# Attention products in pairs, one-tile requests for w_out, and earlier q loads in a fused attention and feed-forward kernel on one Trainium2 core

## The chip, the cores and the metric

The kernel runs on one core of one Trainium2 chip. The metric is the device time of one execution in microseconds (us). Six executions of the kernel before took 951.77 to 955.05 us, with a median of 954.17 us.

The core's engines work side by side and each follows its own list in order: TensorE (PE, whose weight loads are listed as PEld) multiplies matrices, VectorE (DVE) and ScalarE (ACT) do elementwise work, and SyncE's queue (SP) hands out transfers to 16 DMA engines.

## The reference

```python
kv  = einsum('bhsd,bhse->bhde', k, v)            # 8 batches, 8 heads, 576 tokens, 64 wide
out = einsum('bhsd,bhde->bhse', q, kv)
rms = sqrt(mean(out * out, axis=-1) + 1e-6)
x   = (out / rms * g_norm) -> 4608 tokens x 512  # heads side by side
h   = x @ w_in                                   # 512 -> 2048
g   = s * max(h, 0)**2 + b
y   = g @ w_out                                  # 2048 -> 512
```

Everything is float32.

## The kernel before

**Units, chunks, steps.** The 4608 tokens are 36 chunks of 128. Four chunks make a unit of 512 tokens, so there are nine units, u = 0 to 8. For a unit the kernel computes the first matrix product (`mm1`, with w_in) in four steps s = 0 to 3 of 512 hidden columns each, and then the second (`mm2`, with w_out). Both use a Strassen-Winograd scheme: seven products in place of eight, with sums before and after. In a step the seven products are called `x1`, `z2`, `x6`, `y7`, `x5`, `x3`, `y4`. They stand in this order on TensorE, except that `x3` and `y4` of a step are written in the next step: `x1(s)`, `x3(s-1)`, `z2(s)`, `y4(s-1)`, `x6(s)`, `y7(s)`, `x5(s)`. Each is 8 rows of 128 x 256 in the trace. `x1`, `x6`, `x5` and `x3` of a step add up in one PSUM bank, and between them ScalarE copies the running sum out (`keep`, L587: r1 after `x1`, r2 after `x6`, r4 after `x5`; after `x3` it takes a ReLU, L618). So `x6` can't start before r1 is copied, `x5` not before r2, `x3` not before r4. `y7` and `y4` add up in a bank with the tag "y", of which there are two. VectorE adds and squares: after `z2`, after `y4` and after `x5` an addition (L247) and a squared ReLU (L542), after `x3` a square (L621), a sum and a difference. r2 has one buffer, which the addition after `y4(s-1)` has to read before r2 of step s is copied.

For u above 1 the second product has two levels of this scheme. `rest()` writes it out: `p1`, `p2`, `p6`, `p7`, `p4` are second-level products of seven small ones each (numbered 1, 2, 6, 7, 5, 3, 4), `x5_of` and `x3` products of one level. After each small product VectorE scales and adds (`scaled`, L702); product 6 adds to the bank of product 1 and waits until VectorE has read that bank.

**Attention beside it.** While unit u is multiplied, the four chunks of unit u+1 go through attention in parts, each put at a place (s, n) of the steps by `sides(u)`. The places are: n = 0 before `x1`, 1 after `z2`, 2 after `x6`, 3 before `x5`. The parts of a chunk are `turn` (VectorE transposes q, L409), `product` (32 rows of the form 128*32 on TensorE, L439, then the square on ScalarE, L448, and the row sum on VectorE, L450), `norm` (root on ScalarE, L454; reciprocal and multiplication on VectorE, L456 and L458, the latter out of PSUM) and `turn_x` (transpose on VectorE, L483; for every second chunk also the scaling of two chunks by g_norm, four ScalarE instructions, L489). A product has its own PSUM bank (`ps_a`, one buffer). In the units 3 to 7 one chunk a step has its parts at the step's places; the last one has them at (2,3) to (3,2). In unit 2 the fourth chunk's parts fall into `rest()`, at the places `at(0)`, `at(1)`, `at(2)`.

`kv_product` computes k^T v of one batch (144 rows of the form 64*64, L377, into both "t" banks, then four ScalarE copies, L392). One is due in each of the units 1 to 6, at place (1,3).

**Transfers.** Nearly all are issued by SP's queue, in written order. `pump(n)` asks for the next n tiles of w_out (or of k and v) into a ring of seven buffers (L671, L674, L115); each waits until the buffer's last reader is done. `loads` asks for q of two chunks of unit u+2 (L1198) in 16 to 48 pieces. In the units from 3 on, the first half stands at (1,3), behind `kv_product` and its `pump(4)`, and the second at (3,1). Results are stored at L806.

## Time and profile before

| what | value |
|---|---|
| median of 6 executions | 954.17 us (951.77 to 955.05) |
| the profiled execution, its own time | 953.78 us |
| its span | 952.0 us |
| PE / PEld busy | 936.4 us (98%) / 837.7 us (88%) |
| DVE / ACT busy | 643.5 us (68%) / 191.8 us (20%) |
| unit 2, from its first `x1` to the next unit's | 102.25 us |
| units 3, 4, 5, 6, 7 | 102.03, 101.03, 101.07, 101.10, 97.00 us |
| granted TensorE clock in these units | 1.00 |

Times in the timeline count from the span's start. A line gives the start, the busy time, the engine, the source line, the operation, what is written and read, the shape, how many instructions are taken together, and in brackets how long the engine was idle before and what ended that. Unit 2 starts at 247.02 us, unit 3 at 349.27, unit 4 at 451.30, unit 5 at 552.33, unit 6 at 653.40, unit 7 at 754.50.

### The profile page before, as it was taken

The numbers are of one execution on the slowest core, as the hardware profiler recorded it, in microseconds if no ns is written. First come the engines' busy times: TensorE is split into PE (matmuls) and PEld (weight loads), VectorE is DVE, ScalarE is ACT, GpSimd is POOL, SyncE is SP. The second block draws the span as 40 slices with busy tenths as digits, with TensorE's granted clock in tenths as the row PEclk, the third lists the DMA queues.
The fourth block names the chain that finished last, engine by engine and source line by source line (L and its number), as shares of the span: only waits on it lengthen the run. The fifth ranks groups of instructions, "written<-read, shape, count | busy, mean of one in ns | idle before, by whom it ended". The sixth has DMA issues, their size and how long they took to land.

```text
span 952.0 us, 17809 instructions
## 1 busy us (share of the span) xinstructions
PE 936.4 (98%) x7270; PEld 837.7 (88%) x7270; DVE 643.5 (68%) x1167; ACT 191.8 (20%) x366; POOL 6.7 (1%) x18
## 2 busy tenths in 40 slices
PE   7999999999999999999999999999999999999997
PEld 6888888888888998899889988999889988998997
DVE  2789767486567865776568665775578667854684
ACT  2773132101121103200231013101320032001100
POOL 2000000000000000000000000000000000000000
PEclk9999999999999999999999999999999999999999
DMA  9688827578762767165644764375526520653064
GB/s 255 194 283 250 280 78 195 138 218 263 208 174 49 219 184 215 24 196 187 177 108 132 240 181 106 98 240 165 157 52 218 185 90 12 209 181 121 13 221 143
DMA packets 136656, 158.46 MB, mean 166 GB/s; under 512 B 77696, under 2 KB 91776, under 8 KB 136448
## 3 DMA queue, kind: packets, MB, share of 16 engines
q1 hardware_dynamic: 133472, 155.57, 55.1%
q10 hardware_dynamic: 2784, 1.77, 0.8%
q8 instruction: 57, 0.93, 0.4%
q14 instruction: 23, 0.19, 0.1%
q0 software_dynamic: 320, 0.00, 0.0%
HBM read 131.34 MB, written 25.95 MB: 165 GB/s over the span
## 4 chain that ended last, share of the span: by engine, by line
PE 91%; DVE 5%; DMA 2%; ACT 1%; issue 1%; SPq 0%; ACTq 0%; DVEq 0%
PE x_ps L91 41%; PE y_ps L91 27%; PE z_ps L91 9%; PE t_ps L91 8%; PE x_ps L439 3%; PE kv_ps L377 2%; DMA w_raw<-in_moe_w_in_dram 1%; DMA kv_sb<-in_k_dram 1%; DVE sub L250 1%; DVE a L250 1%; DVE b_row L247 1%; DVE xn L458 0%; DMA w_sb<-w 0%; DVE xT L483 0%; ACT w_raw L227 0%
## 5 line engine op out<-in xcount | busy, mean ns | idle before, releaser
L587 ACT COPY r<-x_ps 128x512 f32<-128x512 f32 x96 | 56.2, 586 | 433.9 <-PE x_ps L91 392.2
L91 PE MATMUL y_ps<-xs,wb 128*128 128x256 f32 x512 | 122.3, 382 | 0.3 <-DVE a L247 0.3
L91 PE MATMUL x_ps<-xs,ws 128*128 128x256 f32 x512 | 122.1, 381 | 0.0
L91 PEld LDWEIGHTS y_ps<-xs,wb 128*128 128x128 f32 x512 | 95.7, 190 | 15.1 <-issue 2.4
L91 PEld LDWEIGHTS x_ps<-xs,ws 128*128 128x128 f32 x512 | 96.4, 190 | 14.0 <-issue 1.0
L247 DVE TENSOR_TENSOR a<-y_ps,r 128x512 f32<-128x512 f32 x64 | 44.1, 689 | 76.2 <-ACT r L587 71.3
L91 PE MATMUL x_ps<-xT,wa 128*128 128x256 f32 x384 | 90.3, 381 | 0.1
L91 PEld LDWEIGHTS x_ps<-xT,wa 128*128 128x128 f32 x384 | 71.8, 190 | 11.1 <-issue 1.2
L91 PE MATMUL x_ps<-w_sb,a 128*128 128x256 f32 (+1 forms) x376 | 79.6, 364 | 0.0
L91 PEld LDWEIGHTS x_ps<-w_sb,a 128*128 128x128 f32 x376 | 66.8, 190 | 8.3 <-issue 0.4
L542 DVE SCALAR_TENSOR_TENSOR a<-a 128x512 f32<-128x512 f32 x96 | 66.4, 691 | 3.0
L91 PE MATMUL y_ps<-w_sb,sub 128*128 128x128 f32 x504 | 62.0, 275 | 0.0
L91 PE MATMUL x_ps<-xT,ws 128*128 128x256 f32 x256 | 60.8, 380 | 0.0
L91 PEld LDWEIGHTS y_ps<-w_sb,sub 128*128 128x128 f32 x504 | 60.2, 192 | 0.7
L91 PE MATMUL z_ps<-xT,wa 128*128 128x256 f32 x256 | 60.5, 379 | 0.0
L91 PE MATMUL x_ps<-w_sb,s 128*128 128x256 f32 x256 | 57.9, 380 | 0.8 <-DMA w_sb<-w 0.8
L91 PE MATMUL t_ps<-w_sb,sub 128*128 128x128 f32 x448 | 54.7, 275 | 0.4 <-DVE r L702 0.4
L91 PEld LDWEIGHTS z_ps<-xT,wa 128*128 128x128 f32 x256 | 48.6, 190 | 6.6
L91 PE MATMUL y_ps<-w_sb,a 128*128 128x128 f32 (+1 forms) x360 | 54.0, 299 | 0.0
L91 PEld LDWEIGHTS x_ps<-xT,ws 128*128 128x128 f32 x256 | 47.8, 190 | 6.9 <-ACT r L587 0.9
L91 PEld LDWEIGHTS t_ps<-w_sb,sub 128*128 128x128 f32 x448 | 52.8, 192 | 1.0 <-DVE r L702 0.6
L91 PEld LDWEIGHTS x_ps<-w_sb,s 128*128 128x128 f32 x256 | 47.5, 190 | 7.0 <-issue 1.1
(139 smaller groups left out, 1236.3 us busy)
## 6 DMA issues: line engine op xcount, KB each, us to landing
w_sb<-w SPq DMA_DIRECT2D x147, 512.0 KB, 4.8
w_sb<-w SPq DMA_DIRECT2D x35, 256.0 KB, 2.8
w_raw<-in_moe_w_in_dram SPq DMA_DIRECT2D x8, 1024.0 KB, 8.0
w_raw<-in_moe_w_out_dram SPq DMA_DIRECT2D x8, 1024.0 KB, 5.7
w_sb<-in_k_dram SPq DMA_DIRECT2D x48, 144.0 KB, 2.9
w_sb<-in_v_dram SPq DMA_DIRECT2D x48, 144.0 KB, 3.0
out_dram<-o SPq DMA_DIRECT2D x104, 64.0 KB, 2.3
w<-sub SPq DMA_DIRECT2D x20, 256.0 KB, 4.3
```

What stands on the lines that cost most here:

```text
L91: nc.tensor.matmul(o, lhsT=lhsT, rhs=rhs, start=start, stop=stop, skip_group_check=True)
L247: nc.vector.tensor_tensor(out=o, in0=a, in1=b, op=ALU.add)
L250: nc.vector.tensor_tensor(out=o, in0=a, in1=b, op=ALU.subtract)
L377: nc.tensor.matmul(ps[r][l * HB : l * HB + HB, i, :], lhsT=kv[l][rows, 0, j, :], rhs=kv[l][rows, 1, j, :], start=(j == 0), stop=(j == R - 1),)
L439: nc.tensor.matmul(ps[32 * p : 32 * p + 32, w, :], lhsT=st["qT"][:, p, 32 * w : 32 * w + 32], rhs=bd_kv[(b if w < 2 else b1) % 2][:, p, :] ...
L542: nc.vector.scalar_tensor_tensor(t, t, 0.0, t, ALU.max, ALU.mult)
L587: nc.scalar.copy(st[name], src)
```

## The change

It touches the units 2 to 7.

1. The products of two chunks are written directly behind each other. For this the second of a pair gets another PSUM bank: one of tag "t" for the chunks 13 and 15, one of tag "y" from chunk 17 on. Its row sum becomes a part of its own (`row_sum`), placed later.
2. In the units 3 to 6 the first pair stands directly ahead of `kv_product`, which moves from (1,3) to (1,1). In unit 2, `kv_product` moves to (1,1) too, and the first pair stands at (2,0).
3. The other parts move. From unit 3 on, both `turn_x` of the first pair stand at (2,0) and the last chunk's at (3,1), where it was at (3,2). In unit 2 the parts of two chunks, not one, fall into `rest()`; their products stand at (3,2).
4. The halves of q are asked for at (1,0) and (2,0) from unit 3 on, and the first half at (2,0), before (2,2), in unit 2.
5. In `rest()` nearly every `pump(2)` becomes two `pump(1)`, each behind the small product that is the last reader of a tile. The number of tiles is the same (24).

```diff
-        def product():
+        def product(with_sum=True):
...
-                ps = ps_a.tile([P, NP, P], FP32, name="x_ps", tag="x")
+                pool, tag = (ps_a, "x")
+                if c % 2 and c > 12:
+                    pool, tag = (ps_t, "t") if c < 16 else (ps_f, "y")
+                ps = pool.tile([P, NP, P], FP32, name="x_ps", tag=tag)
...
             nc.scalar.activation(st["xn"], st["x"], AF.Square)
+            if with_sum:
+                row_sum()
+
+        def row_sum():
             st["ss"] = attp.tile([P, H], FP32, name="ss", tag="ss")
             nc.vector.reduce_sum(st["ss"], st["xn"], axis=mybir.AxisListType.X)
...
         def rest():
             p1[1]()
             p1[2]()
+            pump(1)
             step["y4"]()
             p1[6]()
             step["y4_square"]()
             p1[7]()
+            pump(1)
             p1[5]()
-            pump(2)
             step["x3"]()
...
             x5_of(1, lambda: p6["sums"]((7, 3)), lambda: p7["sums"]((5, 6, 7)))
+            pump(2)
             at(2)
-            pump(2)
             p6[1]()
...
             y4_of(0, 3)
+            pump(1)
             y4_of(1, 4)
-            pump(2)
+            pump(1)
             at(("q", 2))
...
         first, second = {}, {}
+        if u + 1 < U:
+            turn, product, norm, turn_x, _, row_sum = chunks_of(u + 1)
+            product = [partial(fn, False) for fn in product]
+        kv = [lambda: kv_product(kv_due[u]), lambda: pump(NP)] if u in kv_due else []
+        q = {half: [partial(loads, u + 2, half)] for half in range(2)}
...
-        if u in kv_due:
-            first[1, 3] = [lambda: kv_product(kv_due[u]), lambda: pump(NP)]
-        for *place, unit, half in (
-            [(1, 3, 2, 1)] if u == 1 else [(2, 2, 4, 0)] if u == 2
-            else [(1, 3, u + 2, 0), (3, 1, u + 2, 1)]
-        ):
-            first.setdefault(tuple(place), []).append(partial(loads, unit, half))
...
-        for s in range(NS):
-            j = s if u > 2 else s - 1
-            if j >= 0:
-                places = [(s, n) for n in range(4)] if s < 3 else [(2, 3), (3, 0), (3, 1), (3, 2)]
-                for place, fn in zip(places, (turn, product, norm, turn_x)):
-                    first.setdefault(place, []).append(fn[j])
         if u == 2:
-            first[3, 3] = [turn[3]]
-            second = {0: [product[3]], 1: [norm[3]], 2: [turn_x[3]]}
+            first = {
+                (1, 1): [turn[0], *kv],
+                (1, 3): [turn[1]],
+                (2, 0): [*product[:2], *q[0]],
+                (2, 1): row_sum[:2],
+                (2, 2): norm[:2],
+                (2, 3): turn_x[:1],
+                (3, 0): [turn_x[1], turn[2]],
+                (3, 1): [turn[3]],
+                (3, 2): product[2:],
+            }
+            second = {0: row_sum[2:], 1: norm[2:], 2: turn_x[2:]}
...
+        else:
+            first = {
+                (0, 1): [turn[0]],
+                (0, 3): [turn[1]],
+                (1, 0): q[0],
+                (1, 1): [*product[:2], *kv],
+                (1, 2): [*turn[2:], *row_sum[:2]],
+                (1, 3): norm[:2],
+                (2, 0): [*turn_x[:2], *q[1]],
+                (2, 1): product[2:],
+                (2, 2): row_sum[2:],
+                (2, 3): norm[2:],
+                (3, 0): [turn_x[2]],
+                (3, 1): [turn_x[3]],
+            }
```

## The prediction

> **What bounds the kernel now.** The page says TensorE: busy for 98% of the span and 91% of the chain that ended last. So only time on TensorE's list counts: gaps in it, and waits that the new order adds.

> ```profile
> PE 936.4 (98%) x7270; PEld 837.7 (88%) x7270; DVE 643.5 (68%) x1167; ACT 191.8 (20%) x366; POOL 6.7 (1%) x18
> ...
> PE 91%; DVE 5%; DMA 2%; ACT 1%; issue 1%; SPq 0%; ACTq 0%; DVEq 0%
> ...
> PEld x_ps L439 <- issue: 10.1, 29, 0.8
> ```

> The last line, from the waits, names the change's target: 29 times the weight loads stand still ahead of an attention product, and nothing visible holds them. Next the timeline of weight loads, in unit 5 and where two products already follow each other, early in the kernel.

> ```profile
> 563.80 1.70 PEld L91 LDWEIGHTS x_ps<-xT,ws 128*128 128x128 f32 x8
> 565.52 1.70 PEld L91 LDWEIGHTS z_ps<-xT,wa 128*128 128x128 f32 x8
> 567.56 0.81 PEld L439 LDWEIGHTS x_ps<-bd_kv,qT 128*32 128x32 f32 x32 [0.33 <-issue]
> 568.57 1.59 PEld L91 LDWEIGHTS y_ps<-xs,wb 128*128 128x128 f32 x8 [0.20 <-issue]
> 570.19 1.70 PEld L91 LDWEIGHTS x_ps<-xs,ws 128*128 128x128 f32 x8
> ...
> 573.95 2.42 PEld L377 LDWEIGHTS kv_ps<-w_sb 64*64 64x64 f32 x144 [0.33 <-issue]
> 576.43 1.59 PEld L91 LDWEIGHTS x_ps<-xs,ws 128*128 128x128 f32 x8
> ...
> 24.24 0.81 PEld L439 LDWEIGHTS x_ps<-bd_kv,qT 128*32 128x32 f32 x32 [0.58 <-DVE qT L425]
> 25.03 0.89 PEld L439 LDWEIGHTS y_ps<-bd_kv,qT 128*32 128x32 f32 x32
> 26.12 3.32 PEld L91 LDWEIGHTS x_ps<-xT,wa 128*128 128x128 f32 x16 [0.20 <-ACT xn L448]
> ```

> A product of the steps takes 1.727 us from start to start (563.80 to 565.52), only 1.61 after a gap. With the attention product, 565.52 to 570.19 is 4.67; two step products alone would be 3.45, so it costs 1.2. In the pair, the second starts 0.79 after the first and the next form 1.09 later: 1.88, against 1.01 (567.56 to 568.57) for one. The second costs 0.87, so a pair saves 1.2 - 0.87 = 0.33 us.

> Last, what stands close to the limit on ACT, DVE and SP.

> ```profile
> 602.13 0.59 ACT L587 COPY r<-x_ps 128x512 f32<-128x512 f32 x1 [4.83 <-DVE a L247]
> 603.42 1.71 ACT L489 ACTIVATE xT<-xT,g_col 128x256 f32<-128x256 f32 x4 [0.71 <-DVE xT L483]
> ...
> 599.92 0.69 DVE L542 SCALAR_TENSOR_TENSOR a<-a 128x512 f32<-128x512 f32 x1
> ...
> 603.00 1.70 PEld L91 LDWEIGHTS x_ps<-xs,ws 128*128 128x128 f32 x8
> ...
> 320.05 0.19 DVE L456 RECIPROCAL inv<-rms 128x8 f32<-128x8 f32 x1
> ...
> 325.04 0.30 DVE L702 SCALAR_TENSOR_TENSOR r<-t_ps,s_col,o 128x128 f32<-128x128 f32 x1
> ...
> 325.39 2.75 PEld L91 LDWEIGHTS t_ps<-w_sb,sub 128*128 128x128 f32 x24 [0.60 <-DVE r L702]
> ...
> 374.96 37.39 SPq L1198 DMA_DIRECT2D q_sb<-in_q_dram  x64
> ...
> 412.92 0.85 SPq L674 DMA_DIRECT2D w_sb<-w  x2
> ...
> 416.94 3.32 PEld L91 LDWEIGHTS x_ps<-w_sb,s 128*128 128x128 f32 x16 [0.92 <-issue]
> ```

> In unit 5's last step r2 is copied at 602.13, and `x5` may start at 603.00: 0.28 to spare. In unit 2's `rest()`, VectorE works without a pause from 320.05, and TensorE already waits 0.60 for its 325.04. In unit 3 the 64 pieces of q keep SP until 412.4, and a w_out tile comes late.

> **The change part by part.**

> *Pairs, units 3 to 7.* Ten pairs by 0.33: -3.3 us. The second bank holds nobody up: the other "y" bank was last read a step earlier.

> *kv behind the first pair, units 3 to 6.* Joined, the product's 0.20 and kv's 0.33 fall away, a gap from form 128*32 to 64*64 comes instead, and one short block (1.61 for 1.727, a gain of 0.12) is lost: 0.41 less the new gap. No row shows that gap; the gaps at these forms' ends run from 0.07 (after kv: 573.95 + 2.42 to 576.43) to 0.33, so the saving is 0.08 to 0.34. No gap at all would give 0.41. Nothing excludes a dearer one: at twice 0.33 it is a loss of 0.25. I take a gap of 0.2, as at a product's other exit: 4 x 0.2 = -0.8 (+1.0 to -1.6). [...] Its k and v are issued by 561.4 in unit 5 and land 3.0 later; kv's new place is at about 568.

> *What kv's old place cost.* At (1,3) its copies and the scaling delayed r4: 0.22 of waiting, 0.12 of it regained, four times: -0.35.

> *The order in step 3, units 3 to 7.* The last `turn_x` moves ahead of the addition after `y4`, and its scaling ahead of r2 on ACT. From 599.92 in unit 5's clock: the squared ReLU takes 0.61, the transpose starts at 600.53 and the scaling 0.73 later (as 602.69 to 603.42), at 601.26, until 602.97; r2 then at 603.0 until 603.63. `x5` starts at 603.68 for 603.00. Less 0.12 regained: 0.56, five times: +2.8. Behind `x5` only r4 and the addition queue up; the addition ends at 607.16, and `y4` would start at 607.2.

> *The order in step 2, units 3 to 7.* Both `turn_x` now stand ahead of r1 on ACT, and `y7` takes the bank that `y4` has just left. From the addition after `x5(1)`, 7.85 us after `y4(0)` starts: squared ReLU 0.72 later, two transposes (0.62, 0.64), scaling (0.73, 1.71), r1 and ReLU (0.48, 0.63), square, sum, difference (0.73, 0.72, 0.61), addition and squared ReLU after `z2` (0.72, 0.62), and the addition after `y4(1)`, 0.69: 9.6, so 17.47 after that start. Nine step products and a pair later (2 x 1.61 + 7 x 1.727 + 0.3 + 1.88) `y7` wants the bank at 17.49. I cost this at nothing, with no reserve: every 0.1 more on that chain is 0.1 per unit.

> *Unit 2.* Two pairs for four singles (one of them was in `rest()`): the step part grows by 2 x (1.2 + 0.87) - 3 x 1.2 = 0.5, and the second pair waits about 0.5 for its transposed q, which VectorE reaches behind step 3's sums. The 0.45 that `y4` waited there at 300.64 goes. So `rest()` begins 0.5 later and wins back 1.2, the product that stood there. But VectorE doesn't: one more row sum takes the place of the 0.80 that it waited for the square, so product 6 of `p2`, which waits for VectorE's reading of product 1, starts 0.3 later than before. Then, ahead of the same step in `p6`, one more norm (0.20 + 0.69, starts 0.84 apart) and transpose (0.63) come before 325.04: 0.3 + 1.5 = +1.8 for the whole unit. Afterwards VectorE has 0.4 to spare between products again, and TensorE leads.

> *q sooner.* The same number of pieces at about 0.58 us; SP's idle wait for kv (369.8 to 372.2 in unit 3) is filled by the first half, so the late tile is asked for 2.8 sooner: 0.92 less 0.12: -0.8, or nothing if the release of its buffer held it instead. The four tiles that stand behind the first half come up to 10 us later; their first reader is 25 us away.

> *Tiles one by one.* Nothing: each transfer waits for its buffer's last reader already (SP's waits name `z_ps` 26 times, 118.8 us), and no store stands between the halves of a pair. Ring slots hide it; without them each tile's 4.8 us to land would show.

> Sum: -3.3 - 0.8 - 0.35 - 0.8 + 2.8 + 1.8 = -0.65. The profiled execution took 953.78, 0.4 below the median; the difference goes on the median: 954.17 - 0.65 = 953.5 us.

> **The rivals.**

> 1. *One of the two jams isn't there.* If ACT does the scaling behind r2, 2.8 go; if VectorE's order in unit 2 has slack that I missed, +1.8 becomes -1.0 (two pairs and the 0.45). Either gives about -3.5: 950.7. For it: only starts and spacings of the old order are known. Against: the scaling is written ahead of r2, and ACT runs in order.
> 2. *Neither jam:* -0.65 - 2.8 - 2.8 = -6.3: 947.9. That is what pairing would give if the side engines had room.
> 3. *Slower: `y7` waits for its bank in step 2.* The chain of 9.6 us has 0.02 to spare. From 0.5 us more per unit the sum passes +1.9; at 0.9, it is +3.8: 958.0. For it: a dozen steps in a row without reserve. Against: each is a duration that repeats to 0.02 in every unit.
> [...]

> **How the numbers follow.** About 0.2% (1.9 us) is what a measurement of this kernel tells from no change. My sum 47%, from 952.3 to 956.1; one jam missing 25%; neither 8%; `y7` waiting for 0.5 or more 18%; pairs saving nothing 2%. Faster 0.33, within 0.2% 0.47, slower 0.20. The range reaches from 950.3, past the first rival, to 956.5, into the third; it leaves out the second, and the ends of the third and fourth.

> **What the profile after would show.** Weight loads of L439 0.79 apart in pairs, kv (L377) behind a pair with a gap of 0.1 to 0.3; in step 3 of the units 3 to 7 `x5` behind an ACT copy of r by 0.6 to 0.7; in unit 2 a wait of over 2 us for a VectorE `r` at product 6 of `p6`; no 0.92 in unit 3. Units 4 to 6 would be about 0.4 shorter, unit 7 about equal. I am wrong if these waits are missing, or if `y7` of step 2 shows one.

## The result and the profile after

The kernel after took 958.02 us in the median of 19 executions (954.22 to 963.01); the kernel before, on the same chips, 953.5 us (951.51 to 955.5). The ratio is 1.005, with a 95% interval of 1.004 to 1.006: slower by 0.5%. The forecast was 953.5 us with a range up to 956.5, so the result lies outside it: -0.65 us was forecast, and +4.5 measured. The profiled execution took 961.43 us, with a span of 959.6 (before: 953.78 and 952.0).

These lines of the page and of the waits of the kernel after answer to the first ones shown of before.

```profile
PE 937.4 (98%) x7270; PEld 843.0 (88%) x7270; DVE 639.2 (67%) x1167; ACT 191.7 (20%) x366; POOL 6.7 (1%) x18
...
PE 79%; DVE 9%; DMA 5%; ACT 3%; issue 2%; SPq 1%; ACTq 0%; DVEq 0%
...
PEld kv_ps L377 <- issue: 8.2, 8, 3.1
PEld x_ps L442 <- issue: 4.8, 13, 0.8
PEld x_ps L91 <- ACT r L594: 2.6, 5, 0.5
PEld t_ps L91 <- DVE r L709: 2.0, 1, 2.0
PEld x_ps L442 <- DVE a L628: 1.7, 5, 0.3
...
PEld y_ps L91 <- DVE a L247: 1.3, 2, 1.1
```

The target was hit: idle time ahead of attention products (L442) that names no releaser fell from 10.1 us in 29 waits to 4.8 in 13. Some of it only changed its name (the 1.7 us put down to VectorE's `a` are new); counted over all releasers, 33 waits with 12.1 us became 23 with 9.2. But the busy times hardly moved, and 7.6 us more went by. Two new waits were expected (ACT's r2 ahead of `x5`, VectorE's r in unit 2). One was not: k^T v (L377) stands still for 8.2 us with no semaphore named (before: 4.9), 3.1 at a time.

Unit by unit, from a unit's first `x1` to the next unit's, as read from the weight loads of each profiled execution (in before, unit 6 starts at 653.37, unit 7 at 754.41 and unit 8 at 852.67, so unit 7 is 98.26 long; the 653.40, 754.50 and 97.00 in the section on the profile before are less exact):

```
us          unit 2   unit 3   unit 4   unit 5   unit 6   unit 7
before      102.25   102.03   101.03   101.03   101.05    98.26
after       105.81   101.49   103.64   100.46   104.73    97.97
difference   +3.56    -0.54    +2.61    -0.57    +3.68    -0.29
```

The units 4, 5 and 6 are written alike, and yet two are 3 to 4 us longer than the third. That was the first thing to explain. The weight loads of units 3, 4 and 6 around the joined k^T v:

```profile
366.07 1.69 PEld L442 LDWEIGHTS x_ps<-bd_kv,qT 128*32 128x32 f32 x64 [0.33 <-DVE a L628]
367.96 2.50 PEld L377 LDWEIGHTS kv_ps<-w_sb 64*64 64x64 f32 x144 [0.20 <-issue]
370.53 1.59 PEld L91 LDWEIGHTS y_ps<-xs,wb 128*128 128x128 f32 x8
...
467.56 1.69 PEld L442 LDWEIGHTS x_ps<-bd_kv,qT 128*32 128x32 f32 x64 [0.33 <-DVE a L628]
469.44 2.34 PEld L377 LDWEIGHTS kv_ps<-w_sb 64*64 64x64 f32 x139 [0.20 <-issue]
474.84 0.20 PEld L377 LDWEIGHTS kv_ps<-w_sb 64*64 64x64 f32 x5 [3.06 <-issue]
475.11 1.59 PEld L91 LDWEIGHTS y_ps<-xs,wb 128*128 128x128 f32 x8
...
673.54 1.72 PEld L377 LDWEIGHTS kv_ps<-w_sb 64*64 64x64 f32 x97 [0.20 <-DMA out_dram<-o]
677.80 0.79 PEld L377 LDWEIGHTS kv_ps<-w_sb 64*64 64x64 f32 x47 [2.54 <-issue]
678.65 3.06 PEld L91 LDWEIGHTS y_ps<-xs,wb 128*128 128x128 f32 x8
```

In unit 3 the join looks as forecast: 0.20 between the pair and k^T v, no gap behind it. In unit 4 the 144 rows break off after 139 for 3.06 us, in unit 6 after 97 for 2.54. In unit 4's pause no other engine of the core worked, only transfers went on, as the windows show (columns: length; busy time and instructions of PE, PEld, DVE, ACT, POOL; granted clock, DMA share, GB/s):

```profile
471.80:474.80 3.00, 0.12 (x7) 0.00 (x0) 0.00 (x0) 0.00 (x0) 0.00 (x0) 1.00 0.56 101
678.60:681.80 3.20, 3.20 (x16) 2.52 (x8) 0.00 (x0) 1.04 (x4) 0.00 (x0) 0.50 0.23 36
326.50:331.00 4.50, 4.44 (x25) 4.45 (x26) 1.81 (x5) 1.51 (x4) 0.00 (x0) 0.62 0.21 72
```

The second window, behind unit 6's pause, runs at half the granted clock: the next eight loads take 3.06 instead of 1.59. The third, behind the wait in unit 2's `rest()`, does so for most of its length.

**What TensorE waits for in a pause.** The page's list of DMA queues (packets, MB, share) has rows for instructions, one of them this:

```profile
q8 instruction: 57, 0.93, 0.4%
```

```
kernel after     piece ends at entry ... of the 424    pause
unit 3           71 and 327                            none
unit 4           157 and 413                           3.06 at 413
unit 5           243                                   none
unit 6           73 and 329                            2.54 at 329
```

With two ends inside, one piece of 256 is used up in 2.0 to 2.7 us (from the first end to the second in these three units). In unit 4 the list passes the first end at 469.75, but the records of the instruction queue show the next transfer starting only at 472.24 (it takes 1.18), and TensorE resumes at 474.84, 1.4 behind the transfer's end and 5.1 after the passing. In unit 6 the passing is at 672.66, the transfer at 675.52 (0.94), and the resumption at 677.80, 1.3 and again 5.1 later. In unit 3, with nearly the same alignment as in unit 6, the transfer starts at 367.19, 0.2 after the passing, and there is no pause. Where a single product stands among the steps, a piece lasts 12 us and more in this trace, and no such pause is seen there.

### The profile page after: what moved, and what is told of

It reads as the page before. It is cut to its first block, busy times and chain, and to the rows that moved or that the text cites. A ratio compares the mean times of both kernels' runs of the same rounds, so it can differ in the third digit from the quotient of the medians.

```text
span 959.6 us, 17790 instructions
## 1 busy us (share of the span) xinstructions
PE 937.4 (98%) x7270; PEld 843.0 (88%) x7270; DVE 639.2 (67%) x1167; ACT 191.7 (20%) x366; POOL 6.7 (1%) x18
## 4 chain that ended last, share of the span: by engine, by line
PE 79%; DVE 9%; DMA 5%; ACT 3%; issue 2%; SPq 1%; ACTq 0%; DVEq 0%
PE x_ps L91 36%; PE y_ps L91 22%; PE z_ps L91 8%; PE t_ps L91 8%; PE x_ps L442 3%; DMA w_raw<-in_moe_w_in_dram 2%; PE kv_ps L377 2%; ACT xT L496 1%; DVE b_row L247 1%; DMA kv_sb<-in_k_dram 1%; DVE xT L490 1%; DVE sub L250 1%; DMA w_raw<-in_moe_w_out_dram 1%; DVE a L250 1%; ACT w_raw L222 1%
## 5 line engine op out<-in xcount | busy, mean ns | idle before, releaser
L91 PE MATMUL y_ps<-xs,wb 128*128 128x256 f32 x512 | 124.0, 386 | 0.7 <-DVE a L247 0.7
L91 PE MATMUL x_ps<-xs,ws 128*128 128x256 f32 x512 | 121.6, 380 | 0.6
L91 PEld LDWEIGHTS x_ps<-xs,ws 128*128 128x128 f32 x512 | 96.8, 190 | 15.7 <-ACT r L594 2.6
L91 PEld LDWEIGHTS y_ps<-xs,wb 128*128 128x128 f32 x512 | 96.8, 192 | 15.4 <-DVE a L247 1.3
L247 DVE TENSOR_TENSOR a<-y_ps,r 128x512 f32<-128x512 f32 x64 | 43.8, 685 | 90.2 <-ACT r L594 59.0
L91 PE MATMUL x_ps<-xT,wa 128*128 128x256 f32 x384 | 89.7, 380 | 0.1
L91 PEld LDWEIGHTS x_ps<-xT,wa 128*128 128x128 f32 x384 | 72.3, 190 | 10.3 <-ACT xT L496 0.5
L91 PE MATMUL x_ps<-w_sb,a 128*128 128x256 f32 (+1 forms) x376 | 79.6, 364 | 0.0
L91 PEld LDWEIGHTS x_ps<-w_sb,a 128*128 128x128 f32 x376 | 66.9, 190 | 8.2 <-issue 0.4
L91 PE MATMUL y_ps<-w_sb,sub 128*128 128x128 f32 x504 | 62.1, 275 | 0.6 <-DVE r L709 0.6
L91 PEld LDWEIGHTS y_ps<-w_sb,sub 128*128 128x128 f32 x504 | 60.2, 192 | 1.5 <-DVE r L709 0.8
L91 PE MATMUL x_ps<-xT,ws 128*128 128x256 f32 x256 | 60.5, 379 | 0.0
L91 PE MATMUL z_ps<-xT,wa 128*128 128x256 f32 x256 | 60.5, 379 | 0.0
L91 PE MATMUL t_ps<-w_sb,sub 128*128 128x128 f32 x448 | 56.3, 280 | 1.8 <-DVE r L709 1.8
L91 PE MATMUL x_ps<-w_sb,s 128*128 128x256 f32 x256 | 57.8, 380 | 0.0
L91 PEld LDWEIGHTS t_ps<-w_sb,sub 128*128 128x128 f32 x448 | 54.4, 197 | 2.4 <-DVE r L709 2.0
L628 DVE TENSOR_TENSOR a<-a 128x512 f32<-128x512 f32 x32 | 22.0, 689 | 50.6 <-ACT a L625 50.6
L91 PEld LDWEIGHTS z_ps<-xT,wa 128*128 128x128 f32 x256 | 48.6, 190 | 6.6
L91 PE MATMUL y_ps<-w_sb,a 128*128 128x128 f32 (+1 forms) x360 | 53.7, 298 | 0.0
L91 PEld LDWEIGHTS x_ps<-xT,ws 128*128 128x128 f32 x256 | 48.1, 190 | 6.2
```

The source lines that it names most:

```text
L91: nc.tensor.matmul(o, lhsT=lhsT, rhs=rhs, start=start, stop=stop, skip_group_check=True)
L247: nc.vector.tensor_tensor(out=o, in0=a, in1=b, op=ALU.add)
L628: nc.vector.tensor_mul(ga["a21", s], ga["a21", s], ga["a21", s])
```

## The experiments

All edits are to the lists in `sides(u)`, except where said. Ratios are to the kernel before.

**1. k^T v apart from the pair.** The kernel after, with k^T v of the units 3 to 6 back at (1,3).

```diff
-                (1, 1): [*product[:2], *kv],
+                (1, 1): product[:2],
...
-                (1, 3): norm[:2],
+                (1, 3): [*norm[:2], *kv],
```

> In units 3 to 6 k^T v goes back to its old place ahead of x5 (behind the first pair's norm), so its 144 short products no longer follow the pair; all else stays. Code theory (TensorE's list is brought in pieces of 256 instructions, and pair and k^T v together, 424 short ones in 4.3 us, use two pieces up faster than the next one comes): the pauses of 2.5 to 3.1 us inside k^T v in units 4 and 6 go, and with them the clock's dip in unit 6; the median falls by 2.5 to 4 us, to 954 to 955.5, and executions lie closer together than the 9 us of the changed kernel. Unit-2 theory (all is lost in unit 2's order): k^T v alone moves nothing but the joint's 0.2 per unit: 958 to 959.

Measured: 954.64 us (12 executions, 952.44 to 957.6), ratio 1.0011 (0.9998 to 1.0023), 3.4 below the kernel after. The units 4 to 6 take 100.69, 100.66 and 100.66 us, all alike, and no pause is left in k^T v:

```profile
474.52 2.45 PEld L377 LDWEIGHTS kv_ps<-w_sb 64*64 64x64 f32 x144 [0.33 <-DMA q_sb<-in_q_dram]
477.04 1.59 PEld L91 LDWEIGHTS x_ps<-xs,ws 128*128 128x128 f32 x8
```

The lines are from unit 4's weight loads. So the join costs 3.4 us (3.7 by the two ratios to before), where the forecast had it save 0.8 plus 0.35. A joined unit without a pause, unit 5 of the kernel after, is 0.20 shorter (100.46): the saving is there, and the pauses cost many times as much. In the same run unit 2 takes 104.21 us (1.96 more than before), with the same wait of 2.0 in `rest()`, but the clock stays at 1.00 through the unit:

```profile
247.19:351.39 104.20, 101.32 (x842) 91.59 (x842) 71.17 (x135) 16.82 (x36) 0.00 (x0) 1.00 0.57 162
```

**2. Unit 2 in its old order.** The kernel after, with unit 2's single products, row sums and `rest()` parts at the places of before, and no bank of tag "t".

```diff
-                if c % 2 and c > 12:
-                    pool, tag = (ps_t, "t") if c < 16 else (ps_f, "y")
+                if c % 2 and c > 16:
+                    pool, tag = (ps_f, "y")
...
+            each = [lambda p=p, r=r: (p(), r()) for p, r in zip(product, row_sum)]
...
-                (1, 1): [turn[0], *kv],
-                (1, 3): [turn[1]],
-                (2, 0): [*product[:2], *q[0]],
...
-                (3, 2): product[2:],
+                (1, 0): [turn[0]],
+                (1, 1): [each[0]],
+                (1, 2): [norm[0]],
+                (1, 3): [*kv, turn_x[0]],
+                (2, 0): [turn[1]],
+                (2, 1): [each[1]],
+                (2, 2): [*q[0], norm[1]],
+                (2, 3): [turn_x[1], turn[2]],
+                (3, 0): [each[2]],
...
-            second = {0: row_sum[2:], 1: norm[2:], 2: turn_x[2:]}
+            second = {0: [each[3]], 1: [norm[3]], 2: [turn_x[3]]}
```

> Unit 2 has the old order, with single products, and all from unit 3 on is as in the changed kernel. Unit-2 theory: 3.5 us or more come back (unit 2 takes 105.8 us in the changed kernel's profile, 102.25 in the old one's), median 953.5 to 954.5. Code theory: only the waits of unit 2 go, 1.8 that I worked out and 0.6 for a late q, in some executions 1.6 for a clock dip: median 955 to 956, and the pauses in k^T v of units 3 to 6 stay.

Measured: 954.85 us (12 executions, 952.44 to 957.15), ratio 1.0003 (0.999 to 1.0017). The median lies between the two theories' ranges, but both have their part: unit 2 takes 102.28 us, so its pairs cost some 3 us as the kernel after has them, and the pauses stay. The list is one entry longer here (14,762): in unit 4 the break comes after 138 rows for 1.94, in the units 3 and 6 for about half a microsecond.

```profile
466.01 2.34 PEld L377 LDWEIGHTS kv_ps<-w_sb 64*64 64x64 f32 x138 [0.20 <-issue]
470.29 0.20 PEld L377 LDWEIGHTS kv_ps<-w_sb 64*64 64x64 f32 x6 [1.94 <-issue]
```

**3. Both.** Edits 1 and 2 together.

```diff
-                (1, 1): [*product[:2], *kv],
+                (1, 1): product[:2],
...
-                (1, 3): norm[:2],
+                (1, 3): [*norm[:2], *kv],
```

> Both: unit 2 in the old order and k^T v apart in units 3 to 6. Code theory together with unit 2's waits: 952 to 953, that is the pairs' 3.3 us less the five waits of x5 (0.4 each) and the late q of unit 3 (about 1). If both losses were the same one seen twice, this would be no better than the better of the two alone.

Measured: 952.12 us (11 executions, 950.42 to 953.25), ratio 0.9976 (0.9965 to 0.9987). With the two costs gone the rest of the change is a gain of 0.24%. Units 4 to 6 are 100.66 us each.

**4. And the last scaling a place later.** Experiment 3 with the last chunk's `turn_x` back where it was, so that ACT copies r2 first.

```diff
-                (3, 1): [turn_x[3]],
+                (3, 2): [turn_x[3]],
```

> As both, and the last chunk's transpose with its four scalings goes back from (3,1) to (3,2), behind the copy of r2, in units 3 to 7. Theory of the wait: the 0.51 us before x5 in step 3 goes, 0.4 net in five units: 2 us below the run with both, 950 to 951, faster than the kernel before by 0.3%. Rival: the transpose delays the sums of the second product by as much: the same as with both.

Measured: 949.76 us (6 executions, 947.98 to 951.96), ratio 0.9951 (0.9935 to 0.9967): faster than both kernels, and a little below the 950 to 951 that was expected. The window of unit 5's stretch of experiment 3 (columns as above):

```profile
551.87:652.53 100.66, 100.55 (x843) 91.48 (x842) 69.05 (x131) 17.11 (x36) 0.00 (x0) 1.00 0.54 158
```

And the windows of units 5 and 7 here:

```profile
550.41:650.69 100.28, 100.28 (x842) 91.56 (x842) 69.06 (x131) 17.23 (x36) 0.00 (x0) 1.00 0.55 158
750.97:848.55 97.58, 97.58 (x698) 89.20 (x698) 69.04 (x131) 16.20 (x32) 0.00 (x0) 1.00 0.40 128
```

TensorE is busy in all of the 100.28 us. ACT's timeline in step 3 of this unit shows r2 copied before the scaling:

```profile
598.94 0.58 ACT L594 COPY r<-x_ps 128x512 f32<-128x512 f32 x1 [4.58 <-PE x_ps L91]
599.85 1.71 ACT L496 ACTIVATE xT<-xT,g_col 128x256 f32<-128x256 f32 x4 [0.32 <-DVE xT L490]
```

In the weight loads of the same stretch `x5` (600.26) follows `y4` with no wait:

```profile
598.53 1.70 PEld L91 LDWEIGHTS y_ps<-xs,wb 128*128 128x128 f32 x8
600.26 1.70 PEld L91 LDWEIGHTS x_ps<-xs,ws 128*128 128x128 f32 x8
```

**5. The list moved by 84 entries.** If pieces of 256 entries cause the pauses, moving the whole list must move them from unit to unit. The kernel after, with 21 small products (four entries each), whose result nobody uses, early in the kernel.

```diff
+    pad_ps = ps_f.tile([P, 2, TB], FP32, name="pad_ps", tag="z", bufs=1)
+    for i in range(21):
+        g = slice(32 * (i % 4), 32 * (i % 4) + 32)
+        nc.tensor.matmul(pad_ps[g, 0, :P], lhsT=ident[:, g], rhs=ident, start=True, stop=True)
```

> The changed kernel with 21 short products added near its start, whose result nobody uses; they put 84 rows into TensorE's list where the engine waits anyway. Code theory: the ends of the 256-row pieces stand 84 rows earlier in every later burst. In the changed kernel's profile they stand 71 and 327 rows into the burst in unit 3, 157 and 413 in unit 4, 243 in unit 5, 73 and 329 in unit 6, and the pauses were at 413 and 329. Now they should stand at 243 in unit 3, 73 and 329 in unit 4, 159 and 415 in unit 5, 245 in unit 6: a pause can come after 329 rows in unit 4 or 415 in unit 5, none over 0.3 us in units 3 and 6. Median about as the changed kernel, 957 to 959. Rival (a transfer that k^T v or its unit waits for): the pauses stay in units 4 and 6 and at the same products.

Measured: 959.03 us (9 executions, 955.33 to 962.36), ratio 1.0052 (1.0034 to 1.007): no faster, but the pauses are elsewhere, at two of the places that had been named beforehand.

```profile
473.08 1.72 PEld L377 LDWEIGHTS kv_ps<-w_sb 64*64 64x64 f32 x97 [0.20 <-DMA out_dram<-o]
475.15 0.79 PEld L377 LDWEIGHTS kv_ps<-w_sb 64*64 64x64 f32 x47 [0.35 <-issue]
...
573.97 2.35 PEld L377 LDWEIGHTS kv_ps<-w_sb 64*64 64x64 f32 x140 [0.20 <-DMA out_dram<-o]
578.80 0.29 PEld L377 LDWEIGHTS kv_ps<-w_sb 64*64 64x64 f32 x4 [2.48 <-issue]
...
678.58 2.51 PEld L377 LDWEIGHTS kv_ps<-w_sb 64*64 64x64 f32 x144 [0.20 <-DMA out_dram<-o]
```

The ends fall 84 entries earlier: 243 in unit 3, 73 and 329 in unit 4, 159 and 415 in unit 5, 245 in unit 6. Unit 5 now breaks off after 140 rows for 2.48, unit 4 after 97 for only 0.35, and unit 6 runs through. Unit 5 of the kernel after had no pause, and unit 6 had one; the code of neither changed. Two shorter stalls (1.99 and 1.35) came in the units 0 and 1 as well, where k^T v stands without a pair but now has two ends inside; the first of them:

```profile
107.08 2.00 PEld L377 LDWEIGHTS kv_ps<-kv_sb 64*64 64x64 f32 x129 [0.33 <-issue]
111.06 0.32 PEld L377 LDWEIGHTS kv_ps<-kv_sb 64*64 64x64 f32 x15 [1.99 <-issue]
```

**6. The join without pairs.** The kernel before, with k^T v directly ahead of the one product at (1,1) in the units 3 to 6.

```diff
-            first[1, 3] = [lambda: kv_product(kv_due[u]), lambda: pump(NP)]
+            first[1, 3 if u < 3 else 1] = [lambda: kv_product(kv_due[u]), lambda: pump(NP)]
```

> The kernel before with one edit: in units 3 to 6 k^T v stands at (1,1), directly ahead of the second chunk's single product. Code theory: 292 + 64 rows in one burst; where two ends of pieces fall into it 2.5 to 4 us apart there is a pause, so up to 2 us per such unit: median 954 to 956, slower than before by 0.1 to 0.2%, though a gap of the weight loads is saved. Rival (joining as such is good, and only the pair's order costs): 0.2 to 0.3 us saved in each of four units, and 0.1 for the wait of x3: 952.5.

Measured: 954.38 us (12 executions, 951.2 to 959.43), ratio 1.0012 (0.9995 to 1.0028): not told from no change. One unit of four pauses, unit 4 (102.72 us), and this time inside the attention product, after 25 of its 32 rows:

```profile
468.28 0.68 PEld L439 LDWEIGHTS x_ps<-bd_kv,qT 128*32 128x32 f32 x25
470.84 0.15 PEld L439 LDWEIGHTS x_ps<-bd_kv,qT 128*32 128x32 f32 x7 [1.88 <-issue]
```

So the pause belongs neither to the pair nor to k^T v, but to the number of the entry. The units 5 and 6, with one end inside, gain 0.2 to 0.3 us. Unit 3 has two ends inside too (after 2 and 258 of 357 entries) and doesn't pause, so two ends in the burst make a pause possible, not certain.

**All pauses together.** The kernel after and the experiments 2, 5 and 6 have ten pauses that name no semaphore inside a burst of these short products. Counted from the start of each kernel's list, every one of them falls at a multiple of 256 plus 193 or 194. A list has 57 such ends, as many as its instruction queue has transfers; experiment 5's longer list (14,845 entries) has 58 of both. So each transfer can be set beside one end. The columns are times in us: when the list passed the end before, when the transfer that belongs to that end ran, when the list reached the next end, and when TensorE resumed.

```
                 end before   transfer          next end   resumed   behind transfer
after, unit 4      469.75     472.24-473.42      471.78     474.84      1.42
after, unit 6      672.66     675.52-676.46      675.26     677.80      1.34
exp. 2, unit 3     362.95     363.18-364.49      365.57     365.98      1.49
exp. 2, unit 4     466.31     468.00-468.88      468.35     470.29      1.41
exp. 2, unit 6     669.80     669.89-671.55      672.39     672.93      1.38
exp. 5, unit 0     107.21     108.61-109.50      109.07     111.06      1.56
exp. 5, unit 1     162.24     163.36-164.32      164.23     165.58      1.26
exp. 5, unit 4     472.20     472.55-473.69      474.80     475.15      1.46
exp. 5, unit 5     574.28     576.33-577.37      576.32     578.80      1.43
exp. 6, unit 4     466.46     468.41-469.31      468.96     470.84      1.52
```

Whatever the pause's length, TensorE resumes 1.26 to 1.56 us behind the end of that transfer. In all ten the list was at the next end less than 1.2 us behind it; at the 551 other ends of the ten traces (each list's first end left out) it came 1.2 us or more behind it, and there is no such pause at any of them. Unit 3 of experiment 6 is one: its transfer had ended at 363.10, and the list came to the next end at 365.66.

**7. One-tile requests alone.** The kernel before, with `rest()` as the change has it.

```diff
             p1[2]()
+            pump(1)
...
-            pump(2)
+            pump(1)
```

> The kernel before with only the second product's requests one by one, each behind a tile's last reader. My step: nothing, within 0.1% of before (953 to 954.5), since each request waits for its buffer on SP's queue anyway. Rival: the earlier request lets a tile land sooner and takes the 0.92 us wait of unit 3 away: 953.

Measured: 953.86 us (11 executions, 952.25 to 955.11), ratio 1.0002 (0.9993 to 1.001). No cost and no gain can be told from no change. (In the profiled execution unit 3 took 103.39 us, since a second w_out tile came late and TensorE waited 1.28 for it; the median doesn't show it.)

**8. q sooner alone.** The kernel before, with the q requests at (1,1) and (2,3) from unit 3 on, and at (2,0) in unit 2.

```diff
-            [(1, 3, 2, 1)] if u == 1 else [(2, 2, 4, 0)] if u == 2
-            else [(1, 3, u + 2, 0), (3, 1, u + 2, 1)]
+            [(1, 3, 2, 1)] if u == 1 else [(2, 0, 4, 0)] if u == 2
+            else [(1, 1, u + 2, 0), (2, 3, u + 2, 1)]
```

> The kernel before with only q asked for sooner: at (1,1) and (2,3) from unit 3 on, at (2,0) in unit 2. My step: the wait of 0.92 us in unit 3's rest() goes, 0.8 net: 953.0. Rival: the tile was held by its buffer, so nothing: 953.8.

Measured: 953.68 us (11 executions, 951.98 to 956.26), ratio 1.0003 (0.9993 to 1.0012). The expected 953.0 did not come; the late w_out tile of unit 3 stayed late. First the issues of SP's queue:

```profile
379.52 1.82 SPq L671 DMA_DIRECT2D w_sb<-w  x4
...
387.87 23.98 SPq L1198 DMA_DIRECT2D q_sb<-in_q_dram  x48
```

And the weight loads, with the wait that should have gone:

```profile
416.51 3.32 PEld L91 LDWEIGHTS x_ps<-w_sb,s 128*128 128x128 f32 x16 [1.06 <-issue]
```

SP stands from 381.3 to 387.87, waiting for the last `turn` of the old order, at (2,3), to give its q buffer free. The next w_out tile is asked for at 411.95, 63.2 us into the unit, as before (412.44, also 63.2). In the kernel after the transposes come earlier, SP goes on, that tile is asked for 58.5 us into the unit, and the wait is gone. So asking for q sooner alone brings nothing here; what the earlier transposes bring alone was not run.

## Why the prediction was wrong, point by point

**Pairs, -3.3: right.** In the units 3 to 7 of the kernel after, the second product of each of the ten pairs starts 0.79 after the first. Experiment 4 has only these pairs and the other small gains in the units 4 to 7: 100.28 for 101.03 to 101.05, and 97.59 for 98.26. Unit 7 has no k^T v, and its -0.67 is two pairs by 0.33.

**kv behind the first pair, -0.8: this is the step that failed.** I bounded it by gaps between forms, and the gap came out as taken: 0.20 ahead of L377, smaller than the 0.33 that this case's rows reach. A unit without a pause gained the 0.20 of the sum. But the step left out what feeds TensorE: 424 entries in 4.3 us, with two ends of pieces inside. With it, the term is +3.4 (958.02 less 954.64, experiment 1), outside the bounds of +1.0 to -1.6 that I had worked out. The rows for it were on the page of before: 57 transfers in the instruction queue, and short products whose weight loads run at about 17 ns each (2.42 us / 144). The stalls counted as "issue" ahead of L377 before (4.9 us, 10 times) gave no warning: seven are gaps of 0.33 between forms, and three, 2.6 us together, lie in the first 13 us. In the profile, the pauses are the reason why units 4 and 6 are long; experiments 1 and 5 show that it is the join, and that the place moves with the list. That TensorE waits there for a piece of its list is shown by the ten pauses: all at ends of pieces, and each over 1.26 to 1.56 us behind the transfer that belongs there. The pauses took 0.35 to 3.06 us, where 288 to 416 weight loads and matmuls follow each other. Why some transfers start 0.1 to 0.4 us after the end before is passed and others 1.1 to 2.9, these runs don't show.

**kv's old place, -0.35: right in mechanism, its size fits.** Before's weight loads show it as four waits of 0.22 us for ACT's r, one ahead of `x3` in each of the units 3 to 6:

```profile
PEld x_ps L91 <- ACT r L587: 0.9, 4, 0.2
```

They are gone in experiment 6, where only k^T v has moved, and in the units 4 to 6 of experiment 1, where k^T v is back at (1,3) but the scaling has moved: either move is enough. The units 4 to 6 gained 0.34 to 0.39 in experiment 1. Two pairs (-0.66) and the `x5` wait of step 3 (+0.38, below) make -0.28 of it; the 0.06 to 0.11 that is left fits the forecast's 0.09 a unit.

**Order of step 3, +2.8: right in place, too large.** ACT does the scaling first and `x5` waits, in the kernel after 0.51 where I had worked out 0.68. ACT's timeline in unit 3:

```profile
401.06 1.71 ACT L496 ACTIVATE xT<-xT,g_col 128x256 f32<-128x256 f32 x4 [4.16 <-DVE xT L490]
402.68 0.56 ACT L594 COPY r<-x_ps 128x512 f32<-128x512 f32 x1
```

And the weight loads of `x5`:

```profile
403.29 1.59 PEld L91 LDWEIGHTS x_ps<-xs,ws 128*128 128x128 f32 x8 [0.51 <-ACT r L594]
```

Net it costs 0.38 a unit (100.66 less 100.28, experiments 3 and 4), so 1.9 for five units, not 2.8. The whole edit brought 2.36 in the medians, since unit 3 had more in it (101.70 against 100.63).

**Unit 2, +1.8: right without the clock.** Experiment 1 measured 104.21 for 102.25, +1.96, with the waits where the forecast has them: product 6 of `p2` and product 6 of `p6`. Counted from the unit's start they begin 0.52 and 1.94 later than before in the kernel after (forecast: 0.3 and 1.8). These are the kernel after's weight loads, 0.81 and 2.03:

```profile
311.29 2.75 PEld L91 LDWEIGHTS y_ps<-w_sb,sub 128*128 128x128 f32 x24 [0.81 <-DVE r L709]
...
326.55 4.38 PEld L91 LDWEIGHTS t_ps<-w_sb,sub 128*128 128x128 f32 x24 [2.03 <-DVE r L709]
```

In the profiled execution of the kernel after, the clock fell to half behind the 2.03, and the 24 loads took 4.38 instead of 2.75: 1.6 more, hence +3.56. What I missed inside the unit is a wait of VectorE for q (its timeline), which put the second product of the first pair 1.46 behind the first (the second pair's wait, taken as 0.5, is 0.25):

```profile
270.58 0.71 DVE L409 STREAM_TRANSPOSE qT<-q_sb 128x512 f32<-128x512 f32 x1 [4.28 <-DMA q_sb<-in_q_dram]
```

**q sooner, -0.8, and the chain of step 2, 0: each right in one half.** The 0.92 in unit 3 is gone (416.50 goes on to 419.18 without a wait). But q of the third and fourth chunk in unit 3 is later than its new `turn` at (1,2): VectorE waits 1.59 at 375.56, the chain that I had found without reserve is pushed, and `y7` waits 1.08. VectorE's timeline:

```profile
375.56 1.30 DVE L409 STREAM_TRANSPOSE qT<-q_sb 128x512 f32<-128x512 f32 x2 [1.59 <-DMA q_sb<-in_q_dram]
```

And the weight loads of `y7`:

```profile
389.10 1.59 PEld L91 LDWEIGHTS y_ps<-xs,wb 128*128 128x128 f32 x8 [1.08 <-DVE a L247]
```

In the units 4 to 7 `y7` doesn't wait at all, so the reckoning of 17.47 against 17.49 held. The fault of the step is that I looked only at who reads the tiles behind q, and not at whether unit 2 could land q in time for the earlier `turn`. Unit 3 gained 0.54, 0.02 and 0.33 us in the kernel after and experiments 1 and 3, where the forecast's terms give 1.2 (1.0 without the join).

**Tiles one by one, 0: right** (experiment 7).

**The rivals.** Number 3, the slower one, gave nearly the measured time (958.0), but its mechanism appears in one unit only; the time agrees by chance. Number 1 and 2 were not the case as the change is written; experiment 4 takes both jams away and comes to 949.76. That pairs save nothing (given 2%) is excluded by their 0.33. None of these was the cause. Without the join the forecast's terms add up to +0.15, and experiment 1 (954.64) lies 0.8 above the median of before measured beside it (953.8). That this is near is in part luck: the jam of step 3 is 0.9 smaller than its term, and unit 3 gained about 1 less.

## What to carry to other kernels

Before short instructions are put side by side, count how many entries the engine's list takes per microsecond: a saving of 0.2 us a join was lost to pauses of up to 3 us in units where a piece of 256 entries was used up in 2.0 to 2.7 us, before the next had come. With longer products between the two bursts no pause was left (experiment 1 keeps the pairs and moves k^T v three products on); but a burst that holds two ends by itself can still pause, as k^T v alone does with its 290 entries in experiment 5 (1.99 and 1.35 us). When copies of the same code take different times and no semaphore is named, number the entries of the list and look whether the breaks lie a fixed number apart, before a wait or a transfer of data is blamed.

## What the runs showed of the hardware that was not expected

**Late instruction pieces.** In the kernel after TensorE passes the end of a 256-entry piece and resumes 5.1 us later where the next transfer starts 2.5 to 2.9 us after the passing; in all ten pauses it resumes 1.26 to 1.56 us behind the transfer's end. At the same entry of the burst (329) it stood 2.54 in one execution's unit 6 and 0.35 in another's unit 4. The times of the kernel after scatter from 954.22 to 963.01, those of experiment 3, which has no such pause in its profile, from 950.42 to 953.25.

**The clock behind a pause.** In the kernel after the granted clock was 0.5 for 3.413 us from 327.04 and from 678.61, behind waits of 2.03 (for VectorE's r) and 2.54. Behind the 3.06 in unit 4 it stayed at 1.00, and behind the same 2.03 of unit 2 in experiment 1 too. Experiment 2 has it from 471.59, and experiment 5 from 329.50 and 578.67. The two starts in one execution lie 351.57 us apart in the kernel after and 249.17 in experiment 5, that is 103 and 73 times 3.413. Each time costs about 1.6 us (in unit 2, 24 loads took 4.38 for 2.75), twice the whole term of the join. What decides when the clock falls, these runs don't show: of the waits 2.03, 2.54 and 3.06 in the kernel after, the longest had no dip.
